# Small values in one tile, fixed places for turned values, and a second kept quarter of K in a two-layer decode kernel

## The chip, the cores and the metric

The kernel runs on one core of a Trainium2 chip. The metric is the device time of one execution in microseconds (us); the median of several executions stands for a kernel. PE is TensorE, DVE is VectorE, ACT is ScalarE, POOL is GpSimd, and SP is SyncE, whose queue issues nearly all loads.

## The reference

One token goes through an attention layer and an MLP, and then through the same attention layer and MLP once more, with the same weights and the same cache. All is float32.

```
B, Sq, D = 1, 1, 512;  H, Sk, Dh = 32, 4096, 128;  F = 1376

def _A_ref(x, k_cache, v_cache, wq, wo):
    q = transpose((x @ wq).reshape(B, Sq, H, Dh), 0, 2, 1, 3)
    scores = einsum("bhqd,bhkd->bhqk", q, k_cache) * (Dh ** -0.5)
    o = einsum("bhqk,bhkd->bhqd", softmax(scores), v_cache)
    return transpose(o, 0, 2, 1, 3).reshape(B, Sq, H * Dh) @ wo

def _B_ref(x, w1, b1, w2, b2):
    return gelu(x @ w1 + b1) @ w2 + b2

x = x + _A_ref(layernorm(x), k_cache, v_cache, wq, wo)
x = x + _B_ref(layernorm(x), w1, b1, w2, b2)
x = x + _A_ref(layernorm(x), k_cache, v_cache, wq, wo)
x = x + _B_ref(layernorm(x), w1, b1, w2, b2)
```

## The kernel before

K and V are 64 MiB each, and both layers need them whole; so the kernel is a long stream of loads with work beside it.

**Tiling.** The 32 heads are 8 groups of 4 (`G`, `J`). A group's K is 128 partitions (the head's 128 values) by 16384 columns: 8 chunks (`C`) of 4 heads by 512 positions. A quarter of a chunk is `U` = 512 columns, 256 KiB. A group's V is as large. The weights `w` hold, for each group, 2048 columns of wo and 2048 of wq.

**Room.** One tile, `arena`, holds all that is loaded. Three homes of 16384 columns (`A_AT`, `C_AT`, `B_AT`) take K and V by turns; `SHARED` lies at the end of the third (its first 6 quarters are the last 6 of that home) and holds the first wq, and at the change of layers W1, W2, the next wq and pieces of K in turn; `SCRATCH` takes exponentials, `PAIR` a pair of wo and wq, `KEPT_K` one quarter of K that stays from the first layer to the second. Small values have tiles of their own: `smalls`, `xcol`, `b1c`, `b2c`, `ident`, `x_wide`, `on_wide` and others; `turned` and `mt` come from a pool with one buffer each.

**A group.** `scores` forms 32 products into `pS`; `exponentials` takes the maximum on DVE and the exponentials on ACT; `weights` turns them on PE; `values` multiplies 3 of V's 8 chunks on PE, and `weighted` does the other 5 on DVE; `sum_up` joins both; `head` and `out_product` apply wo; `next_queries` forms the next group's queries.

**Wide rooms.** `x_wide` has x's four blocks at the start of each quarter of 32 columns. A wide product (L336) loads 128 columns of it at once as weights, from column 2c on, so that rows 0, 32, 64 and 96 of the result hold the queries of the four heads and the other rows hold nothing that is read. `on_wide` serves wo in the same way. `set_x` (L153) fills `x_wide` on DVE and POOL.

**The start.** SP issues the first wq into `SHARED` (L99), the first K, and the first V, in the order of the program. ACT's queue issues x, b1 and b2 (L102 to L104). `first_queries` (L339) forms the queries with four wide products and, between them, the mean (`mean_of`, L173). The first V's home covers the end of that wq, so V's issue waits until PE has read it. b1c is first read at L304, and b2c at L286, both in the MLP.

**The change of layers.** In the last group V comes in four pieces (`LAST`); behind chunks 5, 6 and 7 stands a product with zeros (`idle`, L165), whose result nobody reads. W1, W2, wq and K pieces follow as room comes free: `behind_w2` (L434) issues the two halves of wq behind blocks 1 and 3 of W2. The second layer starts with the group whose K and V still lie in the homes, and takes the groups in reverse. `begin_k(C_AT + 2 * NC, 13)` (L459) loads 13 quarters of the next K, and the kept quarter is the last one.

**Order.** PE and SP work in the order of the program (`keep_in_program_order`); other instructions are ordered by a scheduler. A wait is placed wherever an instruction reads or writes columns that an earlier one writes or reads, taken over all the columns that it touches.

Of the kernel before, what the change touches and what calls it, by code (L numbers as in the profile page):

```python
# [12 lines left out]
F32 = mybir.dt.float32  # L13
# [4 lines left out]
P = 128  # L18
# [3 lines left out]
G = 8  # L22
J = 4
C = 8
FJ = F // J
FB = 11
W1C = FJ * J
EPS = 1e-5
U = 512
NC = 4 * U  # L30
# [7 lines left out]
A_AT, B_AT, C_AT = RING  # L38
# [15 lines left out]
def decode_layers(ctx: ExitStack, tc: tile.TileContext, x, k, v, w, w1, b1, w2, b2, out):  # L54
    nc = tc.nc
    const = ctx.enter_context(tc.tile_pool(name="const", bufs=1))
    work = ctx.enter_context(tc.tile_pool(name="work", bufs=1))
# [7 lines left out]
    def small(name, n=1):  # L65
        if name not in places:
            a = sum(b - a for a, b in places.values())
            places[name] = a, a + n
        a, b = places[name]
        assert b <= 120 and b - a == n  # L70
        return smalls[:, a:b]

    arena = const.tile([P, ARENA], F32, name="arena")

    def at(first, n):
        return arena[:, first : first + n]

    def load(first, src):
        t = at(first, src.shape[-1])
        tc.keep_in_program_order(nc.sync.dma_start(t, src))  # L80
        return t

    def matmul(*a, **kw):
        tc.keep_in_program_order(nc.tensor.matmul(*a, **kw))  # L84
# [7 lines left out]
    def of_w(row, i, n):  # L92
        return w[row][:, NC * i : NC * (i + n)]
# [8 lines left out]
    nc.scalar.dma_start(xcol, x)  # L102
    nc.scalar.dma_start(b1c, b1)
    nc.scalar.dma_start(b2c, b2)  # L104

    ident = ctile("ident", P)
    make_identity(nc, ident)
    negmean = ctile("negmean", 32)
    nc.vector.memset(negmean, -1.0 / D)
    power = ctile("power", 1)  # L110
    nc.gpsimd.memset(power, -0.5)

    zero, one = ctile("zero", 4), ctile("one", 1)
    nc.vector.memset(zero, 0.0)
    nc.vector.memset(one, 1.0)


# [5 lines left out]
    zq = ctile("zq", J, 2 * C - 1)  # L123
    ml, mb = (ctile(n, 32) for n in ("ml", "mb"))
    for t in (zq, ml, mb):
        nc.vector.memset(t, 0.0)

    def of_32(t, n, i=0):
        return t[:, : 32 * n].rearrange("p (c q) -> p c q", q=32)[:, :, i]


    x_wide, on_wide = ctile("x_wide", 32 * J + 6), ctile("on_wide", 32 * J + 3)
    nc.vector.memset(x_wide, 1.0)
    nc.vector.memset(on_wide, 0.0)

    def in_quarters(t, n):
        return t[:, : 32 * J].rearrange("p (j n) -> p j n", j=J)[:, :, :n]
# [1 line left out]
    def pairs(t):  # L139
        return t[:, :8].rearrange("p (c i) -> p c i", i=2)  # L140

    def turned(src, wide=False):

        t = work.tile([P, P], F32, name="turned")
        if wide:
            for j in range(J):
                q = slice(32 * j, 32 * j + 32)
                nc.vector.transpose(t[q], src[q, P * j : P * (j + 1)])  # L148
        else:
            nc.vector.transpose(t, src[:, :P])  # L150
        return t
# [15 lines left out]

    def minus_mean(s, at):
        for j in range(J):
            matmul(at[32 * j : 32 * j + 32, :], negmean, s, start=True, stop=True)  # L170
        return at

    def mean_of(xs, s):  # L173
# [20 lines left out]
    def queries(to, negm, wide=False):  # L194
        qt = turned(to, wide)
        z = zq
        nc.vector.scalar_tensor_tensor(z[:, :, C - 1], of_32(qt, J, 1), negm, of_32(qt, J),
                                       op0=ALU.mult, op1=ALU.add)
        return z
# [6 lines left out]
    def exponentials(sc, nsc):  # L206
        nc.vector.tensor_reduce(ml[:, 0:1], pS, axis=AX.X, op=ALU.max)  # L207
        mt, m, bias = work.tile([P, 32], F32, name="mt"), small("m"), work.tile([P, 32], F32, name="mt")
# [3 lines left out]
        nc.vector.transpose(bias, mb)  # L212
        p = at(SCRATCH, U)
        nc.scalar.activation(p, pS, AF.Exp, bias=bias[:, 0:1], scale=sc, accum_out=ml[:, 0:1])  # L214
        return p

    def weights(p):
        for b in range(4):
            tc.keep_in_program_order(nc.tensor.transpose(  # L219
                pT[:, b].rearrange("p j r -> p (j r)"), p[:, P * b : P * (b + 1)], ident))  # L220
        pt = work.tile([P, P], F32, name="turned").rearrange("p (c j b) -> p c j b", j=J, c=C)
        nc.vector.tensor_copy(pt, pT[:, :, :, :C].rearrange("p b j c -> p c j b"))  # L222
        lt, l, lr, rl = work.tile([P, 32], F32, name="mt"), small("l"), work.tile([P, 32], F32, name="mt"), small("rl")
        nc.vector.transpose(lt, ml)  # L224
        nc.vector.tensor_reduce(l, lt[:, :C], axis=AX.X, op=ALU.add)
        nc.vector.tensor_copy(mb, l.to_broadcast([P, 32]))
        nc.vector.transpose(lr, mb)
        nc.vector.reciprocal(rl, lr[:, 0:1])
        return pt, rl

# [35 lines left out]
                                    op0=ALU.mult)  # L266
        return on

    def head_out(rl, wt, last=False):
        on = head(rl, last)  # L270
        to = pS if last else pO
        out_product(on, wt, to, last)
        return of_32(turned(to, wide=not last), 4)

    def out_product(on, wt, to, narrow=False):
        for d in range(4):
# [115 lines left out]
    for g in range(G):  # L392
        final = g == G - 1
        k_home, v_home = RING[2 * g % 3], RING[(2 * g + 1) % 3]
        acc, pt, rl = group(z, acc, ahead, blocks(k, g, k_home, HALVES if final else ((0, C),)))
        ahead = None
        if g == G - 2:
            nc.scalar.copy(at(KEPT_K, U), at(k_home + NC * C - U, U))
        if g < G - 2:
            t = partly(pt, blocks(v, g, v_home), v_home)  # L400
            pair = load(PAIR, of_w(g % 2, g, 2))
            ahead = t, rl, by_four(pair[:, :NC])
            z = next_queries(xs, negm, by_four(pair[:, NC:]), to=pS)
            continue
        for c, t in blocks(v, g, v_home, LAST if final else ((0, C),)):
            values(c, pt, t, c)
            if final and c > 4:
                idle(pS)
            if g == G - 2:
                for j in range(J):  # L410
                    i = 4 * c + j - KEPT_V // U
                    if i >= 0:
                        nc.scalar.copy(pK[i], t[j])
        if final:
            wo_t = by_four(load(PAIR, of_w(g % 2, g, 1)))
            for i in range(3):
                load_w1(SHARED, i, i + 1)
            own = head_out(rl, wo_t, last=True)
            load_w1(SHARED, 3, 4)
        else:  # L420
            pair = load(PAIR, of_w(g % 2, g, 2))
            acc = add_up(acc, head_out(rl, by_four(pair[:, :NC])))
            wq_t = by_four(pair[:, NC:])
            z = next_queries(xs, negm, wq_t)
    x1, s1 = set_x(own, 1.0, acc, queries=False)

    k_t = []

# [53 lines left out]
    acc = add_up(acc, head_out(rl, by_four(pair[:, NC:])))  # L482
    z = next_queries(xs, negm, by_four(pair[:, :NC]))

    homes, ahead = (A_AT, C_AT, B_AT), None
    for n in range(2, G):
        g, final = G - 1 - n, n == G - 1
# [7 lines left out]
            continue  # L495
        for c, t in blocks(v, g, v_home, LAST):
            values(c, pt, t, c)
            if c > 4:
                idle(pS)
        wo_t = by_four(load(PAIR, of_w(g % 2, g, 1)))  # L500
        for a, b in W1_AT_END:
# [51 lines left out]
```

## Time and profile before

| | |
|---|---|
| median of 3 runs | 676.69 us (675.95 to 678.07) |
| the profiled execution | 675.69 us |
| its span in the trace | 673.9 us |
| PE, DVE, ACT, POOL busy | 398.9, 331.0, 22.5, 4.3 us |
| read from HBM | 285.88 MB |

The profile is of one execution. Its times count from the start of the span. An engine's busy time is not time on the path that sets the end: with 286 MB to move, the rows to look at first are those of the DMA queues. "In us to landing" runs from an issue to the moment when its last byte has arrived.

### The profile page before, as it was taken

Reading aid. Unit: us, or ns where it says so; the run is one execution under the profiler, and the core shown is the slowest. Engines: PE = TensorE matmul, PEld = TensorE weight load, DVE = VectorE, ACT = ScalarE, POOL = GpSimd, SP = SyncE. Lnnn points to the kernel's source line nnn. Section 1 sums busy time; section 2 is a strip of 40 time slices with the busy share of each in tenths; the row PEclk is TensorE's granted clock in tenths of the full one; section 3 lists DMA queues with packets and bytes.
Section 4 is the critical chain, followed back from the end, with each engine's and each line's share of the span. In section 5 each row is a group of like instructions: output and inputs, shape, how many; then the busy total and the mean of one; then the engine's idle time right before and its main releaser. Section 6 shows DMA issues by size and latency. Waiting matters only on the chain. (4 is left out here: it accounts for less than half of the span.)

```text
span 673.9 us, 5767 instructions
## 1 busy us (share of the span) xinstructions
PE 398.9 (59%) x2462; PEld 107.3 (16%) x2462; DVE 331.0 (49%) x483; ACT 22.5 (3%) x48; POOL 4.3 (1%) x21
## 2 busy tenths in 40 slices
PE   4543753647616456376777878738526566284585
PEld 1100110111102111021213222112101112021122
DVE  2059276393682945920112121393672936927531
ACT  0010000000000000001000110000000000000000
POOL 1000000000000000000000000000000000000000
PEclk9657775976869767687979898977759768778698
DMA  9999999999999999999999999999999999999996
GB/s 374 436 437 436 432 433 436 414 454 436 432 436 409 459 433 436 436 433 398 428 414 389 433 446 427 437 441 433 424 428 412 452 436 433 432 428 423 432 409 276
DMA packets 11689, 286.25 MB, mean 425 GB/s; under 512 B 1808, under 2 KB 1808, under 8 KB 3856
## 3 DMA queue, kind: packets, MB, share of 16 engines
q1 hardware_dynamic: 11232, 285.88, 99.0%
q8 instruction: 19, 0.31, 0.2%
q10 hardware_dynamic: 432, 0.01, 0.0%
q14 instruction: 6, 0.05, 0.0%
HBM read 285.88 MB, written 0.00 MB: 424 GB/s over the span
## 5 line engine op out<-in xcount | busy, mean ns | idle before, releaser
L84 PE MATMUL pS<-arena,zq 128*8 128x512 f32 x1024 | 137.4, 697 | 36.2 <-DMA arena<-in_k 31.0
L242 DVE TENSOR_TENSOR arena<-arena,turned 128x10240 f32<-128x10240 f32 x11 | 119.1, 10825 | 41.5 <-DMA arena<-in_v 41.4
L84 PE MATMUL pO<-arena,turned 128*4 128x512 f32 x584 | 98.3, 831 | 53.3 <-DMA arena<-in_v 51.7
L247 DVE TENSOR_TENSOR arena<-arena 128x2048 f32<-128x2048 f32 (+1 forms) x33 | 98.5, 2985 | 0.7
L84 PE MATMUL pO<-arena,one 128*4 128x512 f32 x88 | 20.8, 1037 | 127.6 <-DVE arena L247 127.6
L207 DVE TENSOR_REDUCE ml<-pS 128x1 f32<-128x512 f32 x16 | 11.1, 691 | 153.1 <-PE pS L84 153.1
L84 PEld LDWEIGHTS pS<-arena,zq 128*8 128x8 f32 x1024 | 29.3, 100 | 150.6 <-issue 109.8
L84 PE MATMUL pO<-arena,on_wide 128*128 128x512 f32 (+1 forms) x136 | 49.2, 527 | 4.0 <-DVE on_wide L265 2.7
L84 PE MATMUL pS<-arena,x_wide 128*128 128x512 f32 x88 | 41.1, 609 | 2.7 <-DMA arena<-in_w 2.6
L257 DVE STREAM_TRANSPOSE arena<-pO 128x512 f32<-128x512 f32 x16 | 11.5, 717 | 60.7 <-PE pO L84 60.7
L84 PEld LDWEIGHTS pO<-arena,turned 128*4 128x4 f32 x584 | 16.4, 104 | 119.0 <-issue 115.2
L219 PE MATMUL pO<-ident,arena 128*128 128x128 f32 x64 | 11.1, 300 | 30.4 <-DVE turned L148 16.3
L214 ACT ACTIVATE arena<-pS,mt,smalls 128x512 f32<-128x512 f32 x16 | 12.4, 777 | 493.9 <-DVE mt L212 493.9
L148 DVE STREAM_TRANSPOSE turned<-pO 32x128 f32<-32x128 f32 x64 | 19.8, 309 | 18.1 <-PE pO L84 17.4
L84 PEld LDWEIGHTS pO<-arena,on_wide 128*128 128x128 f32 (+1 forms) x136 | 19.4, 164 | 34.9 <-issue 28.1
L84 PEld LDWEIGHTS pO<-arena,one 128*4 128x4 f32 x88 | 1.2, 84 | 136.7 <-DVE arena L247 136.7
L84 PE MATMUL pO<-arena,x_wide 128*2 128x128 f32 (+1 forms) x88 | 16.4, 400 | 9.6 <-POOL x_wide L162 6.7
L84 PEld LDWEIGHTS pS<-arena,x_wide 128*128 128x128 f32 x88 | 16.1, 194 | 33.1 <-DMA arena<-in_w 17.3
L219 PEld LDWEIGHTS pO<-ident,arena 128*128 128x128 f32 x64 | 7.3, 150 | 43.2 <-issue 25.1
L148 DVE STREAM_TRANSPOSE turned<-pS 32x128 f32<-32x128 f32 x44 | 13.7, 311 | 0.8
L224 DVE STREAM_TRANSPOSE mt<-ml 128x32 f32<-128x32 f32 x16 | 3.4, 212 | 17.0 <-ACT arena L214 17.0
L84 PE MATMUL pO<-arena,smalls 128*2 128x344 f32 x64 | 7.1, 536 | 4.7 <-DMA arena<-in_w 4.0
(79 smaller groups left out, 114.8 us busy)
## 6 DMA issues: line engine op xcount, KB each, us to landing
arena<-in_w SPq DMA_DIRECT2D x13, 2048.0 KB, 11.4
arena<-in_k SPq DMA_DIRECT2D x4, 4096.0 KB, 25.0
arena<-in_v SPq DMA_DIRECT2D x2, 4096.0 KB, 38.9
arena<-in_v SPq DMA_DIRECT2D x3, 2048.0 KB, 43.0
arena<-in_v SPq DMA_DIRECT2D x1, 6144.0 KB, 30.4
arena<-in_w SPq DMA_DIRECT2D x5, 1024.0 KB, 21.6
arena<-in_w SPq DMA_DIRECT2D x6, 688.0 KB, 30.9
arena<-in_v SPq DMA_DIRECT2D x4, 1024.0 KB, 46.4
```

Source lines behind the costliest of these rows:

```text
L84: tc.keep_in_program_order(nc.tensor.matmul(*a, **kw))
L148: nc.vector.transpose(t[q], src[q, P * j : P * (j + 1)])
L207: nc.vector.tensor_reduce(ml[:, 0:1], pS, axis=AX.X, op=ALU.max)
L214: nc.scalar.activation(p, pS, AF.Exp, bias=bias[:, 0:1], scale=sc, accum_out=ml[:, 0:1])
L219: tc.keep_in_program_order(nc.tensor.transpose(pT[:, b].rearrange("p j r -> p (j r)"), p[:, P * b : P * (b + 1)], ident))
L224: nc.vector.transpose(lt, ml)
L242: nc.vector.tensor_tensor(t, t, w.unsqueeze(2).to_broadcast([P, 4 * J * (C - BY_PE), P]), op=ALU.mult)
L247: nc.vector.tensor_tensor(a, a, b, op=ALU.add)
L257: nc.vector.transpose(ot, pO)
```

## The change

- One tile `cells` takes all small values: the identity, `zq`, one wide room of 140 columns and a rest. `x_wide` is that room and `on_wide` is the same room from column 8 on. Values of more than one column go into the gaps of the room (20 columns in each quarter, from column 12 of the quarter on); the first three to ask are b1c, b2c and xcol. The room is set to ones and the rest to zeros before x, b1 and b2 are asked for.
- `turned` has fixed places in the arena: `TURNED`, at the change of layers `SCRATCH`, in the last group of a layer the identity's place; the identity is made again at the second layer's start.
- `KEPT_K` is two quarters; the load at the change is 12 quarters instead of 13, and the copy on ACT takes 1024 columns.
- `idle` behind chunk 6 goes, in both layers.
- The next wq comes in one transfer, behind block 3 of W2.
- In the second layer's first group the next queries are turned inside `exponentials`, to a place in `C_AT`.
- `dynamic_dma_scratch_size` is 128 instead of 256.

```
-ARENA = KEPT_K + U
+TURNED = SHARED + 9 * U
+ARENA = KEPT_K + 2 * U
+ZQ = J * (2 * C - 1)
+WIDE = 32 * J + 8 + 3 + 1
+CELLS = 440
...
-    smalls, places = ctile("smalls", 120), {}
+    cells = ctile("cells", CELLS)
+    ident, zq, wide = cells[:, :P], cells[:, P : P + ZQ], cells[:, P + ZQ : P + ZQ + WIDE]
+    x_wide, on_wide = wide, wide[:, 8:]
...
+    gaps, places = [P + ZQ + 32 * j + 12 for j in range(J)], {}
+    ends = [a + 20 for a in gaps]
...
         if name not in places:
+            fit = [j for j in range(J) if n > 1 and gaps[j] + n <= ends[j]]
+            if fit:
+                places[name] = gaps[fit[0]], n
+                gaps[fit[0]] += n
+            else:
+                places[name] = rest, n
+                rest += n
...
     wq_t = by_four(load(SHARED, of_w(1, 0, 1)))
-    b1c, b2c = ctile("b1c", FB), ctile("b2c", 4)
-    xcol = ctile("xcol", 4)
+    nc.vector.memset(wide, 1.0)
+    nc.vector.memset(cells[:, first_small:], 0.0)
+    b1c, b2c, xcol = small("b1c", FB), small("b2c", 4), small("xcol", 4)
     nc.scalar.dma_start(xcol, x)
     nc.scalar.dma_start(b1c, b1)
     nc.scalar.dma_start(b2c, b2)
...
+    turned_at = [at(TURNED, P)]
...
-        t = work.tile([P, P], F32, name="turned")
+        t = turned_at[0] if to is None else to
...
-            nc.scalar.copy(at(KEPT_K, U), at(k_home + NC * C - U, U))
+            nc.scalar.copy(at(KEPT_K, 2 * U), at(k_home + NC * C - 2 * U, 2 * U))
...
-            if final and c > 4:
+            if final and c in (5, 7):
                 idle(pS)
...
-            own = head_out(rl, wo_t, last=True)
+            own = head_out(rl, wo_t, last=True, home=ident)
...
-        if c in (1, 3):
-            load(SHARED + U * (c - 1), of_w((G - 1) % 2, G - 2, 1)[:, U * (c - 1) : U * (c + 1)])
+        if c == 3:
+            load(SHARED, of_w((G - 1) % 2, G - 2, 1))
...
     negm, z, sc, nsc = first_queries(xs, s, wq_t)
+    make_identity(nc, ident)
...
-            begin_k(C_AT + 2 * NC, 13)
-            k_t.append(at(KEPT_K, U))
+            begin_k(C_AT + 2 * NC, 12)
+            k_t += [at(KEPT_K, U), at(KEPT_K + U, U)]
...
-    p = exponentials(sc, nsc)
     for c in range(4):
         query_block(c, xs, wq_t)
-    z = queries(pO, negm)
+    p = exponentials(sc, nsc, lambda: queries(pO, negm, to=at(C_AT + 21 * U, P)))
```

On PE, the first rows of the program before, with their waits (a DMA wait is named by the lane that its load has; lane 1 is the first wq's here):

```order
L84 MATMUL pO<-arena,x_wide 128x512 [waits DMAHW1_49,DVE_49,Pool_49]
L84 MATMUL pO<-arena,x_wide 128x512
L84 MATMUL pS<-smalls,negmean 32x1 x4
L84 MATMUL pO<-arena,x_wide 128x512 x2
L84 MATMUL pS<-smalls,negmean 32x1 [waits DVE_49]
L84 MATMUL pS<-smalls,negmean 32x1 x3
L84 MATMUL pS<-arena,zq 8x512 [waits DMAHW4_49,DVE_49]
```

The same rows of the changed program; lanes 0 to 3 are those of wq, xcol, b1c and b2c, and `cells` stands for all small tiles:

```order
L108 MATMUL pO<-arena,cells 128x512 [waits DMAHW1_49,DMAHW2_49,DMAHW0_49,DMAHW3_49,DVE_49,Pool_49]
L108 MATMUL pO<-arena,cells 128x512
L108 MATMUL pS<-cells 32x1 x4
L108 MATMUL pO<-arena,cells 128x512 [waits DVE_49]
L108 MATMUL pO<-arena,cells 128x512
L108 MATMUL pS<-cells 32x1 x4
L108 MATMUL pS<-arena,cells 8x512 [waits DMAHW4_49,DVE_49]
```

The first wide product waits for four loads instead of one, and the third for DVE; nothing changes its place.

SP's first rows in the changed program are those of before:

```order
L104 DMA arena<-in_w 128x2048
L104 DMA arena<-in_k 128x16384
L104 DMA arena<-in_v 128x16384 [waits DMAHW0_49,PE_49]
L104 DMA arena<-in_w 128x4096
L104 DMA arena<-in_k 128x16384
```

The first V waits for wq's landing and for PE, as before; the pair of weights and the second K stand behind it.

On SP at the change of layers, before: W2's last pieces, wq's halves, and the pieces of the next K.

```order
L80 DMA arena<-in_w 128x1024
L80 DMA arena<-in_w 128x512
L80 DMA arena<-in_w 128x1024 x2
L80 DMA arena<-in_k 128x2048
L80 DMA arena<-in_k 128x1024
L80 DMA arena<-in_k 128x2048 x3
L80 DMA arena<-in_k 128x6656
```

And in the changed program:

```order
L104 DMA arena<-in_w 128x1024
L104 DMA arena<-in_w 128x512
L104 DMA arena<-in_w 128x2048
L104 DMA arena<-in_k 128x2048
L104 DMA arena<-in_k 128x1024
L104 DMA arena<-in_k 128x2048 x3
L104 DMA arena<-in_k 128x6144
```

Two issues of wq became one, and the last K piece lost 512 columns.

More of the change, by code (lines that the diff above doesn't have):

```diff
@@ L104, in decode_layers @@
     nc.scalar.dma_start(b2c, b2)
-    ident = ctile("ident", P)
     make_identity(nc, ident)
-    negmean = ctile("negmean", 32)
+    negmean = small("negmean")
     nc.vector.memset(negmean, -1.0 / D)
-    power = ctile("power", 1)
+    power = small("power")
     nc.gpsimd.memset(power, -0.5)
-    zero, one = ctile("zero", 4), ctile("one", 1)
-    nc.vector.memset(zero, 0.0)
+    one = small("one")
     nc.vector.memset(one, 1.0)
@@ L122, in decode_layers @@
         nc.vector.memset(t, 0.0)
[L123 to L126, printed above, removed]
+    nc.vector.memset(zq, 0.0)
+    zero = zq[:, 0, :4]
+    turned_at = [at(TURNED, P)]
     def of_32(t, n, i=0):
         return t[:, : 32 * n].rearrange("p (c q) -> p c q", q=32)[:, :, i]
-    x_wide, on_wide = ctile("x_wide", 32 * J + 6), ctile("on_wide", 32 * J + 3)
-    nc.vector.memset(x_wide, 1.0)
-    nc.vector.memset(on_wide, 0.0)
     def in_quarters(t, n):
@@ L140, in pairs, with turned @@
         return t[:, :8].rearrange("p (c i) -> p c i", i=2)
-    def turned(src, wide=False):
-        t = work.tile([P, P], F32, name="turned")
+    def turned(src, wide=False, to=None):
+        t = turned_at[0] if to is None else to
         if wide:
@@ L169, in minus_mean @@
         for j in range(J):
-            matmul(at[32 * j : 32 * j + 32, :], negmean, s, start=True, stop=True)
+            matmul(at[32 * j : 32 * j + 32, :], negmean.to_broadcast([P, 32]), s, start=True, stop=True)
         return at
@@ L192, in query_block, with queries @@
                    start=(c == 0), stop=(c == 3))
-    def queries(to, negm, wide=False):
-        qt = turned(to, wide)
+    def queries(src, negm, wide=False, to=None):
+        qt = turned(src, wide, to)
         z = zq
@@ L204, in scores, with exponentials @@
                    start=(c == 0), stop=(c == C - 1))
-    def exponentials(sc, nsc):
+    def exponentials(sc, nsc, between=None):
         nc.vector.tensor_reduce(ml[:, 0:1], pS, axis=AX.X, op=ALU.max)
-        mt, m, bias = work.tile([P, 32], F32, name="mt"), small("m"), work.tile([P, 32], F32, name="mt")
+        m, bias = small("m"), mt
         nc.vector.transpose(mt, ml)
@@ L212, in exponentials @@
         nc.vector.transpose(bias, mb)
+        if between:
+            between()
         p = at(SCRATCH, U)
@@ L267, in head, with head_out @@
         return on
-    def head_out(rl, wt, last=False):
+    def head_out(rl, wt, last=False, home=None):
         on = head(rl, last)
@@ L272, in head_out @@
         out_product(on, wt, to, last)
-        return of_32(turned(to, wide=not last), 4)
+        return of_32(turned(to, not last, home), 4)
     def out_product(on, wt, to, narrow=False):
@@ L425, in decode_layers @@
     x1, s1 = set_x(own, 1.0, acc, queries=False)
+    turned_at[0] = at(SCRATCH, P)
     k_t = []
```

32 lines of the change are left out of this document (20 added, 12 removed).

## The prediction

> **What bounds the kernel now.** I read the page's head and its forty slices first, then the table of DMA queues.
>
> ```profile
> span 673.9 us, 5767 instructions
> ...
> DMA  9999999999999999999999999999999999999996
> GB/s 374 436 437 436 432 433 436 414 454 436 432 436 409 459 433 436 436 433 398 428 414 389 433 446 427 437 441 433 424 428 412 452 436 433 432 428 423 432 409 276
> ...
> q1 hardware_dynamic: 11232, 285.88, 99.0%
> q10 hardware_dynamic: 432, 0.01, 0.0%
> ```
>
> The 16 DMA engines work in every slice. SP's queue q1 carries 285.88 MB and fills 99.0% of their time; only the first slice and the last are poor. TensorE (59%) and VectorE (49%) have room. So the time is bytes over rate, plus every microsecond in which SP's queue is empty. Next I asked for windows, to see the rate and where it dips (columns: stretch, busy time of PE, PEld, DVE, ACT, POOL, clock of TensorE, DMA share, GB/s).
>
> ```profile
> 24.00:340.00 316.00, 178.63 (x912) 45.65 (x912) 169.46 (x207) 12.03 (x24) 0.00 (x0) 0.75 1.00 432
> 358.00:362.00 4.00, 2.48 (x33) 0.63 (x26) 0.75 (x7) 0.00 (x0) 0.62 (x2) 1.00 0.97 373
> 366.00:370.00 4.00, 3.98 (x93) 2.39 (x92) 0.62 (x4) 0.00 (x0) 0.43 (x3) 1.00 1.03 366
> 382.00:390.00 8.00, 8.00 (x64) 1.56 (x64) 0.00 (x0) 0.00 (x0) 0.00 (x0) 0.81 1.00 424
> ```
>
> In the long first stretch the share is 1.00 at 432 GB/s. At the change of layers, where small weight pieces arrive, two windows dip to 373 and 366. The chain of work that ended last shows the same at the end:
>
> ```profile
> 606.75 45.01 DMA arena<-in_v
> 651.77 0.02 issue
> 651.78 18.03 DMA arena<-in_w
> 669.81 0.04 issue
> 669.86 0.62 PE pS L84 x16
> ```
>
> For the last 63 us it is transfers, and then 4 us of tail. A byte less is a shorter kernel; an engine that works a little longer is not, unless it keeps SP from issuing.
>
> **The start, which the change touches.** Here are the issues on SP's and ScalarE's queues, the rows of the small loads in the table of DMA issues (last column: us from issue to landing), and what PE and DVE do.
>
> ```profile
> 0.73 0.41 ACTq L102 DMA_DIRECT2D xcol<-in_x  x1
> 0.74 0.37 SPq L80 DMA_DIRECT2D arena<-in_w  x1
> 1.16 0.42 SPq L80 DMA_DIRECT2D arena<-in_k  x1
> 1.17 0.46 ACTq L103 DMA_DIRECT2D b1c<-in_b  x1
> 1.66 0.45 ACTq L104 DMA_DIRECT2D b2c<-in_b  x1
> 13.79 0.33 SPq L80 DMA_DIRECT2D arena<-in_v  x1
> ```
> ```profile
> xcol<-in_x ACTq DMA_DIRECT2D x1, 2.0 KB, 5.2
> b1c<-in_b ACTq DMA_DIRECT2D x1, 5.5 KB, 24.1
> b2c<-in_b ACTq DMA_DIRECT2D x1, 2.0 KB, 43.1
> out<-smalls SPq DMA_DIRECT2D x1, 2.0 KB, 1.4
> ```
> ```profile
> 6.00 0.16 DVE L159 SCALAR_TENSOR_TENSOR x_wide<-zero,xcol 128x4 f32<-128x4 f32 x1 [3.47 <-DMA xcol<-in_x]
> 6.72 3.78 PE L84 MATMUL pO<-arena,x_wide 128*128 128x512 f32 x4 [6.72 <-POOL x_wide L162]
> 10.44 0.29 PE L84 MATMUL pS<-smalls,negmean 128*32 128x1 f32 x8
> 10.65 3.10 PE L84 MATMUL pO<-arena,x_wide 128*128 128x512 f32 x4
> 11.06 0.17 DVE L177 SCALAR_TENSOR_TENSOR smalls<-smalls 128x4 f32<-128x4 f32 x1
> 25.25 9.39 PE L84 MATMUL pS<-arena,zq 128*8 128x512 f32 x64 [11.32 <-DMA arena<-in_k]
> 44.74 10.82 DVE L242 TENSOR_TENSOR arena<-arena,turned 128x10240 f32<-128x10240 f32 x1 [4.63 <-DMA arena<-in_v]
> ```
>
> The vector x lands at 0.73 + 5.2 = 5.9, the first queries run from 6.72 to 13.75, and at 13.79 SP issues the first V: it overwrites the first wq, so it waits until PE has read that. The first K lands at 25.25, so V's rows are in the queue 11 us before they are needed, and V lands at 44.74 with no gap.
>
> The two biases land at 1.17 + 24.1 = 25.3 and 1.66 + 43.1 = 44.8. They crawl. The page's 432 packets of q10 are three loads of 128 rows and 16 endings, so each engine has 8 rows of each. One K row is 65,536 bytes; 16 engines at 432 GB/s need 2.43 us for one row each. From x's landing to b1c's are 19.4 us, 8 x 2.43: one small row went by for each K row. b2c took the next 19.5 us beside V's eight. Nobody minded, since b1 and b2 are first used at the MLP.
>
> **The change, part by part.**
>
> *All small values in one tile.* This is the part that I expect to decide. The gaps of the wide room now hold b1c, b2c and xcol (columns 12 to 30 of the first quarter), and the first product of the queries loads columns 0 to 127 of that room as weights. What stands in the gaps only reaches rows that nobody reads, but the order of the changed program shows the wait: that product waits on four DMA semaphores where it waited on one. They are wq, xcol, b1c and b2c. **PE can't start before b2c has landed.** Behind it on PE stand all queries and scores; SP's first V waits for PE; and behind V on SP stand the next pair of weights and the second K. So after K nothing is left in SP's queue.
>
> Step by step. b2c's rows still go one by one beside K's, so most are left over when K is in at 25.25; then nothing competes. Between 0 and the 1.4 us that the lone `out` takes; the rows are queued already, so I take 0.3, and PE starts at 25.55. To the end of the mean's products it took 6.72 to 10.73, 4.01 us: 29.56. The next product now waits for VectorE as well (the xc, sq and mean values also lie in gaps): to the end of L177 at 11.23, 0.50: 30.06. Then two blocks, 3.10 in this trace at a slow clock:
>
> ```profile
> 324.12 3.70 PE L84 MATMUL pO<-arena,x_wide 128*128 128x512 f32 x8 [1.39 <-DVE turned L148]
> 329.47 7.05 PE L84 MATMUL pS<-arena,zq 128*8 128x512 f32 x64 [1.65 <-DVE zq L197]
> ```
>
> Four blocks at full clock take 3.70, so two take 1.85. The scores at 25.25 took 9.39 where warm ones take 7.05: at half rate for h us, h/2 + 9.39 - h = 7.05, so h = 4.7. From 25.55 the clock is up at 30.25, so the blocks take 1.95 (bounds 1.85 and 3.10): 32.01, and SP issues V at 32.05. The Trainium skill (TensorE: Matmul & The Clock Gate, "Part 1: The HAM clock gate (the "warmup" mystery)") has an idle TensorE at half clock until about one busy window of 3.4 us, with a phase that is free; by that alone the blocks would be warm and V's issue 0.1 us earlier, and the 4.7 us here agree with a window and a part.
>
> From issue to landing V needs 8.39 MB / 432 = 19.42 us and a lag. For wq and K together the lag was 25.25 - 0.74 - 9.44/432 (21.85) = 2.66; the lone small `out` took 1.4. I take 2.66, since it is that of loads. V lands at 54.1 where it landed at 44.74: **9.4 us later**. Lowest (25.25, 1.85, 1.4): 7.7. Highest (26.65, 3.10, 2.66): 11.6. From there DMA is full again at 432 GB/s, everything is as before but later, and nothing pays it back.
>
> *A second quarter of a K chunk stays.* 512 x 128 x 4 = 262,144 bytes less in the load at the change of layers: at the 424 GB/s of 382 to 390, **0.6 us** less. The copy on ScalarE doubles:
>
> ```profile
> 288.61 0.62 ACT L398 COPY arena<-arena 128x512 f32<-128x512 f32 x1 [32.23 <-DMA arena<-in_k]
> 299.61 0.78 ACT L214 ACTIVATE arena<-pS,mt,smalls 128x512 f32<-128x512 f32 x1 [10.38 <-DVE mt L212]
> ```
>
> At most 0.62 more, in 10.38 us of idle time. Uncovered it would be those 0.62.
>
> *One idle product less, wq in one transfer.* The idle product, and the two issues of wq:
>
> ```profile
> 352.02 1.12 PE L84 MATMUL pS<-arena,zero 128*128 128x512 f32 x2
> ...
> 364.65 0.80 SPq L80 DMA_DIRECT2D arena<-in_w  x2
> ```
>
> Without the product PE ends the group up to 1.03 us earlier and may release W2's first piece that much earlier; with one issue, wq starts up to 0.47 later (0.80 for both, and an issue takes 0.33, as at 13.79). At best both dips go: (432 - 373)/432 x 4 + (432 - 366)/432 x 4 = 1.16 us gained. At worst 0.47 lost. DMA share in the dips is 0.97 and 1.03, so hardly an engine ran dry: I take 0. On SP the number of issues falls by one, and no wait is added there that a DMA has not long met.
>
> *The rest.* Clearing the tile before x is asked for: one clearing of 140 columns on DVE, 0.17 us, before 0.98. x comes a turn or two of K later (2.4 to 4.9 us), still ahead of b2c, so nothing. The second making of the identity on POOL:
>
> ```profile
> 1.04 0.29 POOL masks.py:199 TENSOR_SCALAR_AFFINE_SELECT ident<-ident 128x128 f32<-128x128 f32 x1
> ...
> 359.17 0.55 POOL L186 TENSOR_TENSOR smalls<-smalls,power 128x1 f32<-128x1 f32 x1 [1.81 <-DVE pS L185]
> ```
>
> About 0.5 us with its clearing, in the 1.81 us that POOL idles before the power; uncovered, 0.5. The turned queries inside the exponentials and the fixed places change no bytes: nothing, within the bounds of the dips. The smaller scratch serves no load in the table of issues, which are all SP's or ScalarE's: nothing.
>
> **The sum.** Against the profiled execution's 675.69 us: + 9.4 - 0.6 = 684.5. The median of the runs is 676.69, 1.0 above the profiled one, so 685.5. Ends: 676.7 + 7.7 - 0.6 - 1.2 = 682.6 and 676.7 + 11.6 - 0.6 + 0.5 = 688.2. A measurement of this kernel tells 0.3% (2.0 us) from no change.
>
> **The rivals.**
>
> *The biases come in time* (not slower). If b2c lands early, PE starts early. The place is the row b1c, the price all of the 9.4, and the point from which it decides: V must be issued by 25.25 - 2.66 = 22.6, so PE must start by 22.6 - 4.01 - 0.50 - 3.10 - 0.04 = 14.9. Then 676.7 - 0.6 = 676.1. That would need several small rows for each K row. Against it stand 24.1 and 43.1 us, one row at a time. The Trainium skill (DMA: Bandwidth & Descriptors, "Queues, rings and completion order") lets each engine go round the queues by whole packets, typically some 9 to 17 descriptors from one before it switches: all 8 rows of a bias would then go in one turn and this rival would win. The trace bears out the going round but not the count, so it gets 5 in 100.
>
> *A slower restart*: the last small rows take as long as a lone load (1.1 more) and the blocks stay at half clock (1.15 more): 685.5 + 2.2 = 687.7. The half clock at 6.72 speaks for it, the 4.7 us against. 15 in 100.
>
> *A quicker restart and filled dips*: lag 1.4 (1.3 less) and 1.16 gained: 685.5 - 2.4 = 683.1. 10 in 100.
>
> *It does only what its words say*: less K and fewer pieces, with the start as before, is 676.1 too. The waits in the changed order speak against it; it shares the 5.
>
> **How the numbers follow.** The forecast, 685.5, has 70 in 100. With both restarts it is 95 for slower by over 0.3%. The 5 left go to no change, but for 1 to faster, should more than the dips be gained beside it. The range 682.6 to 688.2 holds the three slower cases and the bounds of their terms.
>
> **What would show it.** In the profile after: b2c lands at about 25.5; PE's first product starts just behind it, with a DMA of the small loads as its releaser; SP's first V is issued near 32; the second slice falls to about half in DMA and GB/s, and the third starts late; from V's landing near 54 on, every stage stands some 9 us later; q1 carries 285.62 MB. Wrong would be a PE start before 15, or a full second slice.

## The result, and the profile after

| | before | after |
|---|---|---|
| median of 4 runs each | 676.34 us (675.95 to 678.07) | 687.56 us (686.98 to 689.0) |
| profiled execution, its span | 675.69, 673.9 us | 687.38, 685.5 us |
| read from HBM | 285.88 MB | 285.62 MB |

The change makes the kernel slower: ratio 1.0163, with a 95% interval of 1.0143 to 1.0183. It reads 0.26 MB less and takes 11.2 us longer. The head of the page after shows where, in slices of 17.1 us:

```profile
span 685.5 us, 5762 instructions
...
DMA  9399999999999999999999999999999999999997
GB/s 390 161 428 425 429 414 440 432 429 440 418 477 425 428 428 407 447 425 426 431 413 396 413 430 432 411 468 428 426 432 426 439 428 432 430 432 416 432 415 285
...
q1 hardware_dynamic: 11088, 285.61, 97.5%
```

One slice has changed, the second: 3 tenths in place of 9, 161 GB/s in place of 436. All others are as full as before. A window (columns as in the prediction: the last two are DMA share and GB/s, and a row counts where it starts), first before and then after, shows that it is no thinning but a hole:

```profile
25.00:34.00 9.00, 8.75 (x60) 1.88 (x64) 0.00 (x0) 0.00 (x0) 0.00 (x0) 0.72 0.81 350
```
```profile
25.00:34.00 9.00, 7.72 (x20) 2.59 (x23) 0.44 (x4) 0.00 (x0) 0.00 (x0) 1.00 0.00 0
```

In these nine microseconds no row starts; by the packets of the trace the last row ahead of them ends at 24.92, and V's first starts at 35.01. The timeline says why (start, duration, engine, line, operation; in brackets the idle time ahead and what ended it):

```profile
25.72 3.75 PE L108 MATMUL pO<-arena,cells 128*128 128x512 f32 x4 [25.72 <-DMA cells<-in_b]
29.40 0.29 PE L108 MATMUL pS<-cells 128*32 128x1 f32 x8
...
30.02 0.16 DVE L196 SCALAR_TENSOR_TENSOR cells<-cells 128x4 f32<-128x4 f32 x1
...
30.25 3.78 PE L108 MATMUL pO<-arena,cells 128*128 128x512 f32 x4 [0.56 <-DVE cells L196]
...
34.06 0.33 SPq L104 DMA_DIRECT2D arena<-in_v  x1
...
35.80 8.47 PE L108 MATMUL pS<-arena,cells 128*8 128x512 f32 x64 [1.56 <-DVE pS L204]
...
56.36 10.82 DVE L263 TENSOR_TENSOR arena<-arena 128x10240 f32<-128x10240 f32 x1 [6.81 <-DMA arena<-in_v]
```

PE's first product starts at 25.72 where it started at 6.72, released by the load of a bias. V is issued at 34.06 where it was issued at 13.79, and lands at 56.36 where it landed at 44.74: 11.6 us later. The small loads, with us from issue to landing in the last column:

```profile
cells<-in_x ACTq DMA_DIRECT2D x1, 2.0 KB, 4.8
cells<-in_b ACTq DMA_DIRECT2D x1, 5.5 KB, 23.9
cells<-in_b ACTq DMA_DIRECT2D x1, 2.0 KB, 23.6
```

x is as early as before. b1 crawls beside K as before (24.1, now 23.9). b2 took 43.1, and takes 23.6 now that no V stands behind K.

From there on the delay is nearly constant. The table is worked out from the trace: the moment at which the first of the 16 engines reports its part of a transfer as landed, and the difference to before ("later" is the kernel of the first experiment below). It is one profile each; a second profile of the changed kernel (below) differs from the first by up to 0.46 us in these rows.

```
transfer                              before   after           later
first V                                44.18    55.37 +11.19    44.18 +0.00
last piece of V in layer 1            349.69   361.12 +11.43   350.04 +0.35
last piece of the first W2            366.93   378.62 +11.69   367.43 +0.50
wq of layer 2                         369.70   381.71 +12.01   370.90 +1.20
last K piece ahead of the kept ones   381.11   393.16 +12.05   382.21 +1.10
12 quarters of K (13 before)          389.08   400.47 +11.39   389.52 +0.44
last piece of the last W2             667.09   678.84 +11.75   668.16 +1.07
```

### The profile page after: what moved, and what is told of

It reads as the page before. It is cut to its first block, busy times and chain, and to the rows that moved or that the text cites. A ratio compares the mean times of both kernels' runs of the same rounds, so it can differ in the third digit from the quotient of the medians.

```text
span 685.5 us, 5762 instructions
## 1 busy us (share of the span) xinstructions
PE 400.2 (58%) x2458; PEld 107.8 (16%) x2458; DVE 331.0 (48%) x480; ACT 23.0 (3%) x48; POOL 4.9 (1%) x23
## 3 DMA queue, kind: packets, MB, share of 16 engines
HBM read 285.62 MB, written 0.00 MB: 417 GB/s over the span
## 5 line engine op out<-in xcount | busy, mean ns | idle before, releaser
L108 PE MATMUL pS<-arena,cells 128*8 128x512 f32 (+2 forms) x1364 | 197.3, 622 | 31.1 <-DMA arena<-in_k 20.4
L108 PE MATMUL pO<-arena,cells 128*128 128x512 f32 (+5 forms) x382 | 96.8, 618 | 165.1 <-DVE arena L268 125.7
L263 DVE TENSOR_TENSOR arena<-arena 128x10240 f32<-128x10240 f32 x11 | 119.1, 10825 | 43.5 <-DMA arena<-in_v 43.5
L108 PE MATMUL pO<-arena 128*4 128x512 f32 x584 | 97.2, 824 | 55.5 <-DMA arena<-in_v 53.9
L108 PEld LDWEIGHTS pS<-arena,cells 128*8 128x8 f32 (+2 forms) x1364 | 53.8, 105 | 188.6 <-issue 121.3
L108 PEld LDWEIGHTS pO<-arena,cells 128*128 128x128 f32 (+3 forms) x382 | 29.2, 123 | 216.1 <-DVE arena L268 134.8
L108 PEld LDWEIGHTS pO<-arena 128*4 128x4 f32 x584 | 16.3, 103 | 121.2 <-issue 116.2
L167 DVE STREAM_TRANSPOSE arena<-pO 32x128 f32<-32x128 f32 x64 | 19.8, 309 | 19.7 <-PE pO L108 19.1
L235 ACT ACTIVATE arena<-pS,cells 128x512 f32<-128x512 f32 x16 | 12.4, 777 | 496.2 <-DVE cells L231 496.2
L167 DVE STREAM_TRANSPOSE arena<-pS 32x128 f32<-32x128 f32 x44 | 13.7, 310 | 0.8
```

The source lines that it names most:

```text
L263: nc.vector.tensor_tensor(t, t, w.unsqueeze(2).to_broadcast([P, 4 * J * (C - BY_PE), P]), op=ALU.mult)
```

## The experiments

Theory: the first wide product reads 128 columns as weights, the biases lie in these columns' gaps, and this wait alone makes the loss, because SP's next issue hangs on that product. Rivals: another part of the change costs (cleared room, fixed places, one transfer for wq, one idle product less), or the small loads take 24 us by themselves.

**The biases loaded later** (from the changed kernel; both lines go behind the first `first_queries`).

```diff
-    nc.scalar.dma_start(b1c, b1)
-    nc.scalar.dma_start(b2c, b2)
...
     negm, z, sc, nsc = first_queries(xs, s, wq_t, wide=True)
+    nc.scalar.dma_start(b1c, b1)
+    nc.scalar.dma_start(b2c, b2)
```

> The changed kernel with one thing moved: the loads of b1 and b2 (same places in the gaps) are issued behind the first query products, so that these wait for wq and x alone. Theory (the whole loss is the first products' wait on the two biases, which empties SP's queue): the first product starts near 13 us, V is issued near 14.5 us and lands near 44.7 us, the DMA share stays at 1.00 between 25 and 34 us, and the time is the before kernel's less the 0.6 us of the second kept quarter, 675.5 to 676.5 us, ratio 0.998 to 1.000. Rival (the rest of the change costs: cleared room, fixed places for the turned values, the merged wq transfer, one idle product less): the time stays over 680 us although V is issued early.

677.18 us (12 runs), ratio to before 1.0007 (0.9998 to 1.0015). Its timeline:

```profile
6.54 3.78 PE L108 MATMUL pO<-arena,cells 128*128 128x512 f32 x4 [6.54 <-POOL cells L179]
...
14.80 0.33 SPq L104 DMA_DIRECT2D arena<-in_v  x1
...
44.91 10.83 DVE L261 TENSOR_TENSOR arena<-arena 128x10240 f32<-128x10240 f32 x1 [5.85 <-DMA arena<-in_v]
```

```profile
25.00:34.00 9.00, 8.42 (x64) 1.80 (x64) 0.13 (x1) 0.00 (x0) 0.00 (x0) 0.82 0.81 350
```

The hole is gone, and with it the loss: the window from 25 to 34 us moves 350 GB/s, as before. With everything else of the change in place the time is that of before. The rival that another part costs 11 us falls. The first product starts at 6.54, and not near 13 as I had expected. The time is 0.7 over the top of the range that I expected, too: the gain of the kept quarter doesn't show (below).

**The kernel before, with only the biases moved into its `x_wide`.**

```diff
-    b1c, b2c = ctile("b1c", FB), ctile("b2c", 4)
+    x_wide = ctile("x_wide", 32 * J + 6)
+    nc.vector.memset(x_wide, 1.0)
+    b1c, b2c = x_wide[:, 12 : 12 + FB], x_wide[:, 12 + FB : 16 + FB]
...
-    x_wide, on_wide = ctile("x_wide", 32 * J + 6), ctile("on_wide", 32 * J + 3)
-    nc.vector.memset(x_wide, 1.0)
+    on_wide = ctile("on_wide", 32 * J + 3)
```

> The kernel before with nothing changed but the place of the two biases: they lie in the gap of its wide x tile (columns 12 to 26), so that the first wide product reads them as part of its weights. Theory (the wait on the biases alone makes the loss): first product at about 25.6 us, V issued at 32 to 34 us and landing 9.4 to 11.6 us later than before, and the time rises by as much, to 685.5 to 688 us, ratio 1.014 to 1.017. Rival (the biases' place costs nothing by itself and the loss needs the other edits): 676 us, ratio 1.000.

685.48 us, ratio 1.0129 (1.0113 to 1.0145), at the lower edge of what I expected: one part of the change makes most of the loss by itself.

```profile
25.84 3.75 PE L84 MATMUL pO<-arena,x_wide 128*128 128x512 f32 x4 [25.84 <-DMA x_wide<-in_b]
29.52 0.29 PE L84 MATMUL pS<-smalls,negmean 128*32 128x1 f32 x8
29.74 2.35 PE L84 MATMUL pO<-arena,x_wide 128*128 128x512 f32 x4
...
32.13 0.33 SPq L80 DMA_DIRECT2D arena<-in_v  x1
...
54.29 10.82 DVE L243 TENSOR_TENSOR arena<-arena,turned 128x10240 f32<-128x10240 f32 x1 [7.91 <-DMA arena<-in_v]
```

V lands 9.55 later, and the time is 9.1 longer. Here xc, sq and the mean are not in the gaps, so the second pair of products follows without a pause, and it takes 2.35 us. In the changed kernel it took 3.78, behind a pause, and V landed another 2.07 us later.

**The first K in four pieces** (rows of 16,384 bytes in place of 65,536; the wait stays).

```diff
+PIECES = ((0, 2), (2, 4), (4, 6), (6, 8))
...
-        acc, pt, rl = group(z, acc, ahead, blocks(k, g, k_home, HALVES if final else ((0, C),)))
+        acc, pt, rl = group(z, acc, ahead, blocks(k, g, k_home, HALVES if final else PIECES if g == 0 else ((0, C),)))
```

> The changed kernel with the first K transfer in four pieces, rows of 16,384 bytes in place of 65,536, the small loads and the waits as they are. Theory (one small row is taken for each big row that stands beside it on an engine, so that sixteen small rows spread over as many K rows): a row of 0.6 us in place of 2.43, b1 in by about 11 us and b2 by about 16 us, first product near 16 us, V issued near 24 us, before K is in (25.2 us), no empty DMA slice, and the time 676 to 678.5 us. Rival (the small loads need some 24 us by themselves, whatever stands beside them): first product at 25.7 us again and 687.5 us.

```profile
cells<-in_x ACTq DMA_DIRECT2D x1, 2.0 KB, 4.7
cells<-in_b ACTq DMA_DIRECT2D x1, 5.5 KB, 9.3
cells<-in_b ACTq DMA_DIRECT2D x1, 2.0 KB, 13.9
```

The three were issued at 1.04, 1.49 and 1.97, so they land at 5.7, 10.8 and 15.9: two steps of 5.1 us, 8 x 0.63 each. A row of 16,384 bytes takes 2.43 / 4 = 0.61. So an engine took one row of a bias for each K row beside it; the biases' time was their neighbours' row length and not their own. PE starts at 16.03, V is issued at 22.12 and lands at 45.45. The time is 678.96 us, ratio 1.0031 (1.0021 to 1.0042), 0.5 over the range that I gave: 0.7 of the 2.6 us is V's landing, and the rest arose at the change of layers, where this profile's wq and small K pieces landed up to 1.7 us later still than in the first experiment's. Why there was not tried.

**The first wq in the place of the pair of weights** (`PAIR`), so that the next pair of weights, and not V, waits for the products.

```diff
-    wq_t = by_four(load(SHARED, of_w(1, 0, 1)))
+    wq_t = by_four(load(PAIR, of_w(1, 0, 1)))
```

> The changed kernel with the first wq fetched into the pair's place, so that the first V transfer no longer waits for the first products (they read wq from where V goes) and the next pair of weights waits for them instead. The products still wait for both biases. Theory (one small row is taken for each big row, and the loss is the empty queue, wherever the products' wait falls): V's rows now stand right behind K's, so b2's eight rows go one for each V row instead of in a bunch and b2 lands near 43 us, as in the kernel before; the first product starts near 44 us, the queue runs empty at 45 us instead of 25, and the end comes 8 to 11 us later than before, 685 to 688 us. Rival (b2 lands near 25 us whatever follows K): products from 25.7 to 34 us, pair and K issued at 34 us while V is still landing, no empty queue, 676 to 677 us.

```profile
cells<-in_b ACTq DMA_DIRECT2D x1, 5.5 KB, 24.1
cells<-in_b ACTq DMA_DIRECT2D x1, 2.0 KB, 43.2
```
```profile
45.33 3.75 PE L108 MATMUL pO<-arena,cells 128*128 128x512 f32 x4 [45.33 <-DMA cells<-in_b]
...
51.88 0.33 SPq L104 DMA_DIRECT2D arena<-in_w  x1
```
```profile
45.00:52.00 7.00, 6.11 (x24) 2.21 (x24) 0.55 (x5) 0.00 (x0) 0.00 (x0) 1.00 0.00 0
98.00:104.00 6.00, 4.12 (x25) 1.43 (x27) 4.14 (x13) 0.87 (x2) 0.00 (x0) 1.00 0.51 177
```

V is now issued at 1.65 and stands right behind K, and b2 takes 43.2 us again, beside V's rows. The hole has only moved, from 25 to 45 us: 691.63 us, ratio 1.0247 (1.0206 to 1.0288). That is 15.3 us and not the 8 to 11 that I expected. The next V can't be issued until the first scores are done, at 60.74, and the queue runs thin a second time: the issue behind it comes at 99.98, when that V has landed at 99.3 (the last window above, with half the DMA share). Moved to this place, the wait costs more.

**The pause taken out** (xc and sq leave the gaps; early single values take places there).

```diff
+EARLY = ("negmean", "power", "one", "x_sum", "sc", "nsc", "l", "rl")
...
-            fit = [j for j in range(J) if n > 1 and gaps[j] + n <= ends[j]]
+            fit = [j for j in range(J) if (n > 1 or name in EARLY) and name not in ("xc", "sq") and gaps[j] + n <= ends[j]]
```

> The changed kernel with xc and sq taken out of the gaps (eight single values that are written early, or after the first products, take places there instead), so that the third and fourth wide product of the start no longer wait 0.56 us for VectorE. The wait on the biases stays. Theory (the pause broke TensorE's busy stretch, and the clock then stayed at half until 38.7 us, through the second pair of products): products run without a pause from 25.7 us, the second pair starts at 29.7 us and takes 1.9 to 2.5 us in place of 3.78, V is issued at 31.8 to 32.4 us in place of 34.06, and the time falls by 1.7 to 2.4 us, to 685.2 to 686 us. Rival (the clock rises at its own time and the pause has no part in it): the second pair takes about 3.75 us, V is issued at 33.5 us, 0.56 us earlier, time 687 us.

```profile
25.66 3.75 PE L109 MATMUL pO<-arena,cells 128*128 128x512 f32 x4 [25.66 <-DMA cells<-in_b]
29.35 0.29 PE L109 MATMUL pS<-cells 128*32 128x1 f32 x8
29.57 2.71 PE L109 MATMUL pO<-arena,cells 128*128 128x512 f32 x4
...
32.30 0.33 SPq L105 DMA_DIRECT2D arena<-in_v  x1
```

686.22 us, ratio to before 1.0137 (1.0121 to 1.0154). The second pair of products took 2.71 us, over the 1.9 to 2.5 that I expected. By the trace V is issued 1.76 us earlier than in the changed kernel; the intervals of the two ratios overlap, so the times alone don't tell them apart. To see whether the pause or chance made the difference, both kernels were profiled once more, unchanged.

> The changed kernel unchanged, for a second profile of its start. Theory (the pause of 0.56 us before the second pair of products keeps TensorE at half speed): the second pair takes about 3.78 us again and the scores behind it more than 8 us. Rival (the moment at which the speed rises has a phase of its own in each execution): the second pair takes anything from 1.9 to 3.8 us, and V is issued up to 1.8 us earlier than 34.06.

> The kernel of e5_mean_out unchanged, for a second profile. Theory (without the pause TensorE reaches full speed some 5 us after its first product): the second pair takes 1.9 to 2.8 us again and the scores 7.05. Rival (the phase of each execution): it may be up to 3.7 us this time.

First the changed kernel again, then the one without the pause:

```profile
30.25 3.66 PE L108 MATMUL pO<-arena,cells 128*128 128x512 f32 x4 [0.56 <-DVE cells L196]
...
33.94 0.33 SPq L104 DMA_DIRECT2D arena<-in_v  x1
```
```profile
29.68 3.05 PE L109 MATMUL pO<-arena,cells 128*128 128x512 f32 x4
...
32.76 0.33 SPq L105 DMA_DIRECT2D arena<-in_v  x1
```

687.30 and 687.49 us, one run each. The pair without the pause took 3.05 us, over the 1.9 to 2.8 that I expected; the one with it took 3.66, but the scores behind it took 7.05, where I had expected more than 8. V landed at 56.28 and 54.95, so 1.33 us earlier without the pause, and yet the end was no earlier: what the pause costs in the whole time is not shown. The section on the hardware puts these together with the other profiles.

**Where the kept quarter's gain went.** Four kernels, each from that with the later biases: one kept quarter as before; wq in halves as before; the third idle product back; both of the last two.

```diff
-ARENA = KEPT_K + 2 * U
+ARENA = KEPT_K + U
...
-            nc.scalar.copy(at(KEPT_K, 2 * U), at(k_home + NC * C - 2 * U, 2 * U))
+            nc.scalar.copy(at(KEPT_K, U), at(k_home + NC * C - U, U))
...
-            begin_k(C_AT + 2 * NC, 12)
-            k_t += [at(KEPT_K, U), at(KEPT_K + U, U)]
+            begin_k(C_AT + 2 * NC, 13)
+            k_t.append(at(KEPT_K, U))
```
```diff
-        if c == 3:
-            load(SHARED, of_w((G - 1) % 2, G - 2, 1))
+        if c in (1, 3):
+            load(SHARED + U * (c - 1), of_w((G - 1) % 2, G - 2, 1)[:, U * (c - 1) : U * (c + 1)])
```
```diff
-            if final and c in (5, 7):
+            if final and c > 4:
...
-            if c in (5, 7):
+            if c > 4:
```

> The kernel of e2_bias_later (biases loaded behind the first products) with one kept K quarter, as before the change, so that the third group of the first heads of layer 2 fetches 13 quarters and not 12 from memory. Theory (a transfer of 262,144 bytes less is worth its time in the full queue, 0.6 us): that transfer (26,624-byte rows) lands 0.6 us later relative to the one ahead of it, the end 0.6 us later, 677.8 us against 677.2. Rival (the gain is lost again in gaps behind it, because the next K transfer's issue hangs on TensorE and not on the queue): same end, 677.2 us.

> The kernel of e2_bias_later with the wq of layer 2 fetched in two halves again, as before the change, the first behind W2's second product block, the second behind the fourth. Theory (one transfer, issued behind the fourth block at 366.57 us, reaches engines that run dry at about 367.4, which costs some 0.7 us): the first half is issued near 365.7 us, the gap between the last W2 row and the first of wq shrinks from about 1.0 to 0.3 us, and the end comes 0.4 to 0.7 us earlier, near 676.6 us, at or just under the kernel before. Rival (merging costs nothing, as I put it in the prediction): 677.2 us.

> The kernel of e2_bias_later with the third idle product put back in the last groups of both layers. Theory (the second layer's start waits on TensorE at the change of layers, and one idle product less lets the clock there fall to half between 361 and 365 us, which moves every issue behind it by 0.9 us): with the product back the clock there is full as in the kernel before, wq is issued near 365.7 instead of 366.57 us, and the end comes 0.3 to 0.9 us earlier, 676.3 to 676.9 us. Rival (the half clock there comes from the phase of the clock's own windows, and the product does not matter): 677.2 us, with the slow stretch still at 361 to 365 us.

> The kernel of e2_bias_later with both put back, wq in two halves and the third idle product: what is left of the change is the one tile, the fixed places and the second kept quarter. Theory (the two edits at the change of layers lose what the quarter gains): the best of the set, 675.5 to 676.2 us, 0.2 to 0.9 us under the kernel before. Rival (neither matters): 677.2 us, ratio 1.001.

| kernel (12 runs each) | median | ratio to before |
|---|---|---|
| biases later | 677.18 us | 1.0007 (0.9998 to 1.0015) |
| one kept quarter | 677.58 us | 1.0011 (1.0001 to 1.0022) |
| wq in halves | 676.53 us | 0.9999 (0.9988 to 1.0011) |
| third idle product | 676.61 us | 1.0001 (0.9992 to 1.001) |
| both back | 676.23 us | 0.9996 (0.9987 to 1.0005) |

The medians stand in the expected order, but all five intervals overlap; the times settle none of the three edits. The traces say more. From the last K piece to the end of the long transfer behind it the first engine to report needs 7.31 us with 12 quarters (biases later) and 7.92 with 13 (one kept quarter): the quarter is worth 0.61 us there. In the kernel with both back it needs 7.50. Against it, from the end of the last W2 piece to that of wq it needs 2.49 to 3.77 us in the ten profiles with one transfer (mean 3.21) and 2.74 to 3.00 in the four with halves (mean 2.87), where a full queue needs 2.43. By the means merging costs 0.3 us, though the ranges overlap, and the changed kernel alone has 3.09 in its first profile and 2.49 in its second. If the means hold, some half of the gain is spent shortly before it is made. The rest drifts away behind it, + 0.36 in the table from there to the last W2 (+ 0.63 with the biases later); what causes that stays open.

The idle product's expectation failed, although its median lies in the range that went with it. The half speed at the change of layers was there with the product, too. Eight products of 128x344, first in the kernel with later biases, then with the product back, then in a second profile of the former:

```profile
361.38 1.33 PE L108 MATMUL pO<-arena,cells 128*2 128x344 f32 x8 [0.34 <-DMA arena<-in_w]
```
```profile
359.94 1.33 PE L108 MATMUL pO<-arena,cells 128*2 128x344 f32 x8 [0.91 <-DMA arena<-in_w]
```
```profile
361.44 0.76 PE L108 MATMUL pO<-arena,cells 128*2 128x344 f32 x8 [0.91 <-DMA arena<-in_w]
```

> The kernel of e2_bias_later unchanged, for a second profile. Theory (the half clock between 359.7 and 365 us, at the change of layers, is the phase of the clock in that one execution and no property of the program): this profile may have full clock there, 0.76 us for eight products of 128x344 in place of 1.33, with wq issued 0.9 to 1.1 us earlier and the end 0.5 to 1 us earlier. Rival (it belongs to the program): 1.33 us again at the same two places.

Same program, 0.76 in place of 1.33 us: the half speed there is no property of the program. (The kernel with both back has 0.76, too.) wq was issued 0.54 us earlier, but this profile's span is 675.8 us and the first one's 675.2, so the half speed doesn't set the end by itself.

No version was found that beats the kernel before by more than its measurement can tell. The one with both put back and the biases later is 11 us faster than the changed kernel and level with the one before. The biases in the tile's rest, behind the wide room, would be the plainest way out of the wait; that was not run.

## Why the prediction was right, and where its sizes were off

- **The wait.** Right, and shown from both sides: taking it away brings the time back (1.0007), and adding it alone to the kernel before makes 1.0129.
- **One small row for each K row.** Right for b1. By the packets of the trace after, its 128 rows start in eight groups of 16, 2.42 us apart, from 7.31 to 24.85, and b2's 128 all start between 24.34 and 24.91, when K's rows are nearly through. The row length decides, as the four pieces show. The rival that the biases come in time falls here, and with it, for the biases, the count of the Trainium skill (DMA: Bandwidth & Descriptors, "Queues, rings and completion order"), some 9 to 17 descriptors from one queue before an engine switches: eight rows of a bias needed eight turns. It isn't so for every small load: x's 128 rows started in one group, 4.82 to 5.48, between wq's rows and K's. What decides between the two stays open.
- **x.** I had it a turn or two of K later. It landed at 5.84, before at 5.93; nothing hung on it.
- **PE's start.** 25.55 forecast, 25.72 measured: once K is in, b2's remaining rows cost next to nothing, not the 1.1 us of the slower rival.
- **To the second pair.** 4.01 + 0.50 us forecast, 30.25 - 25.72 = 4.53 measured.
- **The second pair of blocks: the mis-sized term.** 1.95 us forecast, with an upper bound of 3.10; 3.78 measured. I had taken it that full speed comes 4.7 us after the first product, from one row of before in which PE ran without a pause. The change itself puts a pause of 0.56 us into that stretch, which I priced as 0.50 us of waiting and no more. This is 1.83 of the 2.23 us by which V's landing was forecast too early; it is the half of the rival "slower restart" that came true. Without the pause the term would have been too small as well, by 0.4 to 1.15 us (2.35 to 3.10 in four profiles): one row was no measure of a moment that differs between executions.
- **The lag of the restart.** 56.36 - 34.06 - 19.42 = 2.88 us, against 2.66 forecast. V's first row started 0.95 us behind the issue, and the first row on each engine took 3.01 to 3.52 us, where a row in the full stream takes 2.42.
- **V's landing.** + 9.4 us forecast. The terms above add 0.17 + 0.02 + 1.83 + 0.22, less 0.01 for SP's issue behind the pair, = 2.23, and + 11.6 is what came. That this is just the top of my bounds (56.38, measured 56.36) is luck: the pair and the lag went 0.68 and 0.22 over theirs, and PE's start stayed 0.93 under its own.
- **The time.** 687.56 us came for 685.5 forecast, and lies nearer to the 687.7 of the rival "slower restart". That is luck as well: its one half, the pair, came larger than it was priced (1.83 for 1.15), and the other, 1.1 us for the last small rows, did not come.
- **The kept quarter.** 0.6 forecast; the table shows 12.05 - 11.39 = 0.66 gained there. But the sum took it off the end, and there it is gone: V landed 11.6 us later, and the span is 11.6 us longer.
- **wq in one transfer.** Taken as 0, with 0.47 lost at worst. In the table + 0.32 from W2 to wq, and 0.3 by the means of all profiles, but the second profile of the changed kernel has 0.28 less than before: whether the one transfer costs something is not settled, and what there is lies within the bounds that I had set.
- **Nothing pays it back.** Right: the delay of 11.19 us at the first V is 11.75 at the last W2.

## What to carry to other kernels

Sharing a tile is not free where an instruction reads a range with gaps: here it waited for everything that was loaded into the gaps, read or not. Ask of each such wait what is queued behind it, since the price is not the late instruction but the queue that runs empty behind it; the hole in this full DMA stream was not paid back. A small load issued behind long rows can take its neighbours' time, as b1 and b2 did, so put it ahead of them, as x was, or where nobody waits for it.

## What the hardware showed that I had not expected

TensorE's speed after a start has a phase that differs between executions, and a short pause can cost the products behind it more than its length. The column of the granted clock reads 1.00 throughout the hole after, where products take double, because the trace's records of the clock begin only at its first rise, at 38.71 us there; so speed is read here from durations (two wide products take 1.85 us at full speed, 3.7 at half). The second pair took, without a pause ahead of it, 3.10 (before), 2.35, 2.71 and 3.05 us: a pair that takes t was at half speed for 2 x (t - 1.85), so full speed came 4.9 to 6.4 us after the first product. With the pause of 0.56 us, in ten profiles, it took 1.98 or 1.99 us in three (the K in pieces, the wq apart, the second profile of the later biases) and 3.66 to 3.78 in seven (both profiles of the changed kernel, and the later biases with all that was built on them), and nothing between. The three had full speed by the time the pause was over; the seven missed it for all or nearly all of the pair, and the changed kernel's first profile until inside the scores behind it (8.47 us for 7.05).

The clock records agree. Full clock begins 4.7 to 6.2 us after the first product without the pause, 2.8 to 4.0 us after it in the three, and 8.0 to 9.0 us in the seven but for 13.0 in the changed kernel's first profile. In all 14 profiles the length of every record but the last is a whole multiple of 3.413 us, so within an execution the clock changes on a grid of that length, and the products start anywhere in it. Counted back from the rise, each of the seven has a window with the pause in it, in which PE was busy for 0.83 or 0.84 of the time, and at its end the clock did not rise. The share of busy time alone doesn't settle it: with the K in pieces a window with 0.82 of it was enough.

The Trainium skill (TensorE: Matmul & The Clock Gate, "Part 1: The HAM clock gate (the "warmup" mystery)") has a free-running window of about 3.4 us that must be busy before the clock rises; these runs agree, if a window with the pause in it doesn't count. That reading fits the two groups and the records; how long a pause a window bears was not tested.
